# A layer norm feeding a 2-D Fourier filter and an MLP: features dealt to partitions, W1 on two queues, filter loads behind the normalized tiles

## The chip, the cores and the metric

The kernel runs on one core of a Trainium2 chip. The metric is the time of the program on the device in microseconds, the median of several runs. A profile of one execution gives a span (first to last instruction), which is a little shorter than the time.

## What is computed

Only A_x is used as input data (B_x is not read). With x of 2048 rows by 640:

```python
xn = _layernorm(x, axis=-1)                       # (x - mean) / sqrt(var + 1e-5), rows of 640
# A: spectral filter
X = jnp.fft.rfft2(xn.astype(jnp.float32), axes=(-2, -1)) * (w_r + 1j * w_i)     # 2048 x 321
yA = jnp.fft.irfft2(X, s=(2048, 640), axes=(-2, -1))
# B: MLP
h = _gelu(jnp.einsum("bsd,df->bsf", xn, w1) + b1)       # 640 -> 1536
yB = jnp.einsum("bsf,fd->bsd", h, w2) + b2              # 1536 -> 640
return x + yA + yB
```

All inputs and the output are bf16.

## The kernel before

**Tiles.** The 2048 rows are dealt to 16 tiles of 128: partition p holds rows 16p to 16p+15, tile c the c-th of each. X, the normalized and transposed xnT, W1, W2, the hidden gT, the filter Wf and the tables all stay in SBUF.

**Normalization, on VectorE, tile by tile.** Two statistics of 320 columns each (L483), an aggregate (L485), a small add (L492), the power -1/2 on POOL (L493), and the normalization itself (L511), which writes one of two pair buffers (`p_xn`, tiles 2k and 2k+1 share one). Tiles 0 to 5 are then transposed by TensorE (L527) and copied to xnT by VectorE or ScalarE; tiles 6 to 15 (`BYDMA`) by a transposing DMA on SyncE's queue (L518), which waits for the pair's normalizations. A pair buffer is free for the pair after next when its transposes have landed.

**Fourier part.** VectorE folds each pair with adds and subtractions (L539, L543); TensorE multiplies by gtab (the `aps` of a pair: ten matmuls, five a tile), and the result goes to XV. When all pairs are there, the forward transform along the width runs in six groups (etab; `bps`), then in four double pairs the small 32x32 matmuls with mtab (`cps`), the filter's products and sums on VectorE (L648, L652; they need the whole of Wf), the small matmuls with ntab (`dps`), and transposing DMAs (L673) back to XV. The inverse transform along the width (getab, `eps`) follows in six groups, VectorE unfolds (L704, L709), and one matmul with htab a tile adds the result to the tile's output.

**MLP.** The first layer runs in blocks of tiles, `BLOCKS`: tiles 0, 1, 2-3, 4-7, 8-11, 12-15. For each block and each of 12 chunks of 128 features, five matmuls accumulate in a PSUM bank, with the W1 columns as weights (the stationary operand) and xnT as the moving one, so 128, 256 or 512 columns wide; ScalarE applies Gelu with the bias column b1col (L581). The second layer (L732) takes gT as weights and W2 as the moving operand, 24 matmuls a tile (512 + 128 columns, 12 chunks). Eight tiles (`KEEP`) are summed early and parked in X or xnT (L741); for the others the htab matmul accumulates in the same bank. VectorE adds the rest (L750), and the outputs go out by an accumulating DMA on POOL (L757), over a copy of x that POOL has sent to the output ahead of them (issue at L376; it waits for the whole of Wf and for the last transposed tile), or for tiles 14 and 15 directly by SyncE (L754).

**Loads.** `load` (L375 to L380; all issues are shown at L376) puts every input on SyncE's queue: X tile 0, the first of W1's three parts (`W1P`: chunks 0-2, 3-6, 7-11), the identity, X tile 1, W1's second part, b1 (12 partitions of 128), X tiles 2-3, W1's third part, gtab, X tiles 4 to 15, W2 in four loads of three chunks, the tables etab, mtab, b2, ntab, getab, htab, and then the filter in 34 loads of 16 partitions with runs of 321 elements (`load_w`). b1 is turned into a column by a matmul with the identity (L469) and copied by ScalarE (L470).

**What sets the order.** Each engine's order is written out in `ORDER`, a text that a planner outside the kernel produced: operation number, engine letter, PSUM or buffer slots. `Sched.arrange` reads it, `Sched.sync` works out the semaphore waits from what each operation reads and writes (`deps`), and `Sched.emit` writes them. The arguments `prio`, `rate`, `issue`, `gate` and `hard` are for the planner: neither `sync` nor `emit` reads them.

Of the kernel before, what the change touches and what calls it, by code (L numbers as in the profile page):

```python
# [253 lines left out]
8s 2a 1d 3g 0d 4g 5g 6g 7p:0 9s 10s 11s 12s 13s 70d 14s 69d 15s 71d 16s 72a 17s 73a 74d 136d:0 18s 76d 137p:1 19s 139p:0 75d 140p:2 20s 141a 138d 77d 21s 257p:4 78d 258p 263p:5 79g  # L254
22s 264p 67p:6 269p:7 23s 68a 270p 81d 24s 266p:6 271a 83d 267p 259a 254p:7 25s 80d 268a 255p 260p:4 265a 261p 26s 142d 272p:6 256a 273p 82d 27s 262a 143p:5 145d:0 274a 28s 275p:4
146d 144a 276p 281p:7 84d 29s 284p:6 285p 277a 282p 147d:0 299p:5 30s 286a 300p 149d 293p:4 283a 294p 31s 311p:6 150d 301a 85d 312p 296p:7 148d 32s 295a 86d 297p 152p:0 87g 313a
89d 33s 317p:5 298a 318p 91d 151p 319a 305p:4 34s 154d:1 306p 153a 278p:6 100d 302p:7 155p:5 35s 99d 303p 279p 108d 304a 36s 280a 101d 156d 323p:7 307a 324p 37s 314p:6 157d 315p
325a 290p:5 291p 115d 316a 158p:4 38s 292a 124d 287p:7 288p 320p:6 39s 159d 321p 289a 308p:5 309p 322a 129d 338p:4 40s 310a 161d:0 356p:7 332p:6 96d 41s 357p 121d 341p:5 42s 358a
97d 342p 333p 160d 343a 359p:7 43s 98d 360p 334a 163d:1 102d 335p:5 165d 44s 103g 120d 361a 336p 350p:6 104d 337a 45s 351p 122d 184d:0 347p:7 352a 348p 128d 46s 326p:5 349a 164d
327p 185s 186d 353p:6 328a 354p 116d 344p:7 88d 355a 345p 339p 117d 47s 90d 346a 329p:5 92d 330p 340a 112d 187s 598p:6 331a 732d 613p:4 107d 48s 93d 109d 614p 94d 113d 95g 49s 123d  # L260
615p 114d 50s 172d:1 118d 169d 51s 119g 599p 125d 130d 126d 162d 52s 127g 170p:3 132d 166p:0 53s 175d:0 171a 167p 105d 600p 54s 168a 176d 106d 601p 55s 180d:0 110d 178d 111g 179d
# [529 lines left out]
```

## Time and profile before

| | |
|---|---|
| median of 3 runs | 160.04 us (159.53 to 160.74) |
| the profiled execution's time | 159.53 us |
| its span | 157.7 us |
| busy: TensorE (PE) | 146.2 us, 93% of the span |
| busy: VectorE (DVE) | 109.8 us, 70% |
| busy: ScalarE (ACT) | 77.5 us, 49% |
| busy: GpSimd (POOL) | 21.1 us, 13% |
| DMA | 20.71 MB, mean 131 GB/s |

Rows of the profile have the line of the kernel, the engine, the operation, output tile <- input tiles, the shape, and a count; a row of the order in time starts with start and duration in us and ends, in brackets, with the idle time just before it and what ended it. A row that merges several instructions has the time from the first's start to the last's end. PEld is TensorE's loading of weights, which overlaps its matmuls; SPq is SyncE's queue, whose rows are the issues of DMAs. The chain of waits follows the work that ended last back to the start.

### The profile page before, as it was taken

The numbers are of one execution on the slowest core, as the hardware profiler recorded it, in microseconds if no ns is written. First come the engines' busy times: TensorE is split into PE (matmuls) and PEld (weight loads), VectorE is DVE, ScalarE is ACT, GpSimd is POOL, SyncE is SP. The second block draws the span as 40 slices with busy tenths as digits, with TensorE's granted clock in tenths as the row PEclk, the third lists the DMA queues.
The fourth block names the chain that finished last, engine by engine and source line by source line (L and its number), as shares of the span: only waits on it lengthen the run. The fifth ranks groups of instructions, "written<-read, shape, count | busy, mean of one in ns | idle before, by whom it ended". The sixth has DMA issues, their size and how long they took to land.

```text
span 157.7 us, 4031 instructions
## 1 busy us (share of the span) xinstructions
PE 146.2 (93%) x1703; PEld 89.5 (57%) x1720; DVE 109.8 (70%) x234; ACT 77.5 (49%) x137; POOL 21.1 (13%) x34
## 2 busy tenths in 40 slices
PE   7879899967998799999999999999999999999993
PEld 7669887633454355544454554454456656665663
DVE  2549899998419544699866976961108997989552
ACT  3448976231487678696773553438663310220100
POOL 1001010522000004000000000000000247144520
PEclk9968999996999999999999999999999999999999
DMA  4999999998455537910062025044440079834953
GB/s 116 313 389 399 364 360 260 169 126 152 96 128 132 125 83 209 386 78 4 4 123 44 4 56 119 0 87 84 83 87 0 0 87 94 114 42 50 130 69 88
DMA packets 31337, 20.71 MB, mean 131 GB/s; under 512 B 19288, under 2 KB 29656, under 8 KB 31320
## 3 DMA queue, kind: packets, MB, share of 16 engines
q1 hardware_dynamic: 28728, 15.55, 40.5%
q0 software_dynamic: 2592, 4.92, 17.1%
q8 instruction: 13, 0.21, 0.6%
q14 instruction: 4, 0.03, 0.1%
HBM read 13.58 MB, written 5.24 MB: 119 GB/s over the span
## 4 chain that ended last, share of the span: by engine, by line
PE 69%; DVE 10%; SPq 9%; DMA 7%; issue 2%; ACT 1%
PE ps L385 69%; SPq L376 7%; DVE stats L483 4%; DMA W<-in_B_w_dram 4%; DMA xnT<-T 3%; SPq L518 2%; DVE T L539 1%; DVE T L543 1%; DVE T L511 1%; ACT XV L396 1%; DVE mv L485 1%; PE ps L527 1%; DVE xnT L719 1%; ACT gT L581 0%; DVE xnT L397 0%
## 5 line engine op out<-in xcount | busy, mean ns | idle before, releaser
L385 PE MATMUL ps<-xnT,W 128*128 128x512 bf16 (+2 forms) x360 | 60.0, 320 | 5.7 <-DMA xnT<-T 3.6
L385 PE MATMUL ps<-W,gT 128*128 128x128 bf16 (+3 forms) x382 | 54.8, 292 | 1.5 <-issue 1.1
L385 PEld LDWEIGHTS ps<-xnT,W 128*128 128x128 bf16 x360 | 30.4, 102 | 27.2 <-issue 5.8
L581 ACT ACTIVATE gT<-ps,b1col 128x512 bf16<-128x512 f32 (+2 forms) x72 | 36.3, 547 | 16.5 <-PE ps L385 15.5
L385 PEld LDWEIGHTS ps<-W,gT 128*128 128x128 bf16 x396 | 29.8, 98 | 22.6 <-issue 2.2
L757 POOL DMA_DIRECT2D out_dram<-W x14 | 12.2, 932 | 78.8 <-DVE W L750 78.8
L396 ACT ACTIVATE Wf<-ps 128x960 bf16<-128x960 f32 (+1 forms) x7 | 6.2, 893 | 24.3 <-PE ps L385 24.3
L483 DVE BATCH_NORM_STATS2 stats<-X 128x6 f32<-128x320 bf16 x32 | 14.2, 480 | 5.6 <-DMA X<-in_A_x_dram 5.6
L397 DVE CAST Wf<-ps 128x960 bf16<-128x960 f32 (+1 forms) x5 | 5.1, 1024 | 10.8 <-PE ps L385 10.8
L648 DVE TENSOR_TENSOR T<-Y,Wf 128x1288 bf16<-128x1288 bf16 x16 | 12.3, 822 | 0.0
L511 DVE TENSOR_SCALAR T<-X,mv,rstd 128x640 bf16<-128x640 bf16 x16 | 6.9, 435 | 5.6 <-DMA xnT<-T 5.6
L397 DVE CAST Xb<-ps 128x960 bf16<-128x960 f32 (+1 forms) x6 | 6.7, 1124 | 5.0 <-PE ps L385 5.0
L493 POOL TENSOR_TENSOR rstd<-ve,mhalf 128x2 f32<-128x2 f32 (+1 forms) x8 | 6.0, 750 | 31.1 <-DVE ve L492 31.1
L396 ACT ACTIVATE XV<-ps 128x1280 bf16<-128x1280 f32 (+1 forms) x8 | 9.3, 1156 | 1.5 <-PE ps L385 1.5
L543 DVE TENSOR_TENSOR T<-T 128x512 bf16<-128x512 bf16 (+1 forms) x32 | 8.7, 314 | 0.6 <-PE ps L385 0.6
L396 ACT ACTIVATE Y<-ps 128x644 bf16<-128x644 f32 x8 | 5.7, 708 | 6.9 <-PE ps L385 6.9
L397 DVE CAST Y<-ps 128x644 bf16<-128x644 f32 x8 | 6.6, 823 | 3.5 <-PE ps L385 3.4
L396 ACT ACTIVATE Xb<-ps 128x960 bf16<-128x960 f32 (+1 forms) x6 | 6.8, 1139 | 3.7 <-PE ps L385 3.7
L385 PE MATMUL ps<-getab,XV 32*128 32x160 bf16 (+1 forms) x128 | 7.6, 242 | 0.0
L741 DVE TENSOR_TENSOR X<-ps,b2bc 128x640 f32<-128x640 f32 x7 | 5.7, 821 | 2.4 <-PE ps L385 2.4
L539 DVE TENSOR_TENSOR T<-T 128x640 bf16<-128x640 bf16 x16 | 7.3, 482 | 0.1
L385 PEld LDWEIGHTS ps<-getab,XV 32*128 32x128 bf16 (+1 forms) x128 | 6.4, 147 | 1.6 <-DMA XV<-gtab 0.4
(49 smaller groups left out, 124.6 us busy)
## 6 DMA issues: line engine op xcount, KB each, us to landing
out_dram<-in_A_x_dram POOLq DMA_DIRECT2D x4, 640.0 KB, 7.1
W<-in_B_w_dram SPq DMA_DIRECT2D x5, 480.0 KB, 10.8
X<-in_A_x_dram SPq DMA_DIRECT2D x7, 320.0 KB, 9.2
out_dram<-W POOLq DMA_DIRECT2D x14, 160.0 KB, 3.7
Wf<-in_A_w_r_dram SPq DMA_DIRECT2D x15, 80.2 KB, 5.7
Wf<-in_A_w_i_dram SPq DMA_DIRECT2D x15, 80.2 KB, 2.7
W<-in_B_w_dram SPq DMA_DIRECT2D x1, 800.0 KB, 7.9
W<-in_B_w_dram SPq DMA_DIRECT2D x1, 640.0 KB, 6.3
```

The lines of the kernel that those rows point to most:

```text
L376: o = K.op([(q, 1.0 if q == "pool" else issue)], prio, lambda e, _: e.dma_start(dst, src), reads=reads, writes=[buf], after=after, dma=(nb ...
L385: ins = e.matmul(o_, lhsT=lw, rhs=rh, start=st, stop=sp_, skip_group_check=True)
L396: return e.activation(dst(), src(), ACT.Copy, scale=scale)
L397: return e.tensor_copy(dst(), src())
L483: st_ops.append(K.op([("dve", 0.393)], pr, lambda e, _, c=c, h=h: e.bn_stats(stats[:, c, 6 * h:6 * h + 6], view(X, c * D + H2 * h, [[1, H2 ...
L493: K.op([("pool", 0.65)], 400 + pr, lambda e, _, a=a, b=b: e.tensor_tensor(out=rstd[:, a:b], in0=ve[:, a:b], in1=mhalf[:, a:b], op=ALU.pow) ...
L511: o = K.op([("dve", 0.356)], pr, lambda e, _, c=c, n=n, xnv=xnv: e.tensor_scalar(out=xnv(n, 0, [[1, D]]), in0=view(X, c * D, [[1, D]]), sc ...
L539: K.op([("dve", 0.39)], pr, lambda e, _, k=k, op=op, xnv=xnv, x1v=x1v: e.tensor_tensor(out=x1v(H2 * k, [[D, 2], [1, H2]]), in0=xnv(0, 0, [ ...
L543: ring_ops.append(K.op([("dve", 0.333 if w == 128 else 0.136)], pr, lambda e, _, op=op, x1v=x1v, xfv=xfv, o_=o_, o0=o0, o1=o1, w=w: e.tens ...
L581: K.op([("act", act_us(128 * nt, 1) + 0.02)], pr + PRIO["gelu"], lambda e, _, c0=c0, nt=nt, fc=fc, hps=hps: e.activation(gT[:, fc, 128 * c ...
L648: filt_ops.append(K.op([("dve", 0.738)], pr, lambda e, _, k=k, Y=Y, TB=TB, pair=pair: e.tensor_tensor(out=view(TT, TB.slot * 8 * KP + k * ...
L757: last.append(K.op([("pool", 0.9)], 450, lambda e, _, c=c, os_=os_: e.dma_start(ov[:, c, :], view(W1, OST + os_.slot * D, [[1, D]]), accum ...
```

## The change

- Features are dealt to partitions differently: inside each of W1's three parts, which have 3, 4 and 5 chunks, chunk j of partition p is now feature 128a + p(b-a) + j, where a and b are the part's ends in chunks. W2 is loaded in three loads, in which a partition reads one run of 3, 4 or 5 rows of 640. b1 is loaded as a column, in three loads on POOL's queue, and widened to f32 by a copy on POOL. The matmul and the ScalarE copy for b1 are gone. The W1 columns that serve as weights of one matmul are now 3, 4 or 5 elements apart.
- W1's second and third parts are loaded by ScalarE's queue.
- On SyncE's queue the identity and X tile 1 come ahead of W1's first part; getab and htab come behind the filter loads.
- `FILTER` gives five filter loads (numbers 0, 8, 14, 20, 26) a gate on the normalization of tiles 7, 9, 11, 13 and 15.
- Some of the planner's rates differ, and `ORDER` is written anew for all engines.

The diff, with `ORDER` cut to its first lines:

```diff
 ORDER = """
-8s 2a 1d 3g 0d 4g 5g 6g 7p:0 9s 10s 11s 12s 13s 70d 14s 69d 15s 71d 16s 72a 17s 73a 74d 136d:0 18s 76d 137p:1 19s 139p:0 75d 140p:2 20s 141a 138d 77d 21s 257p:4 78d 258p 263p:5 79g
...
+8s 2a 1d 3g 0d 5g 4g 6g 7p:0 9s 22g 10s 20a 11s 24g 21a 12s 13s 69d 26g 14s 70d 15s 71d 76d 72a 16s 73a 74d 17s 136d:0 75d 18s 139p:1 140p:0 19s 77d 141a 78d 137p:2 23s 79g 138d
...
@@ -292,6 +292,7 @@
 CHAIN = "b0 b1 c00 c01 b2 c10 c11 d00 d01 b3 b4 c20 c21 d10 d11 b5 c30 c31 d20 d21 d30 d31".split()
 XASPLIT = [((0, 1, 2, 3, 4),)] * 7 + [((0, 1), (2, 3, 4))]
 WARM = (42, 10)
+FILTER = {7: 0, 9: 8, 11: 14, 13: 20, 15: 26}
 
 
 def bass_parallel_sum__spectral_gfnet__dense_activation_gelu__prompt_kernel(
@@ -311,8 +312,6 @@
     xv = A_x[0].rearrange("(p c) d -> p c d", c=16)
     ov = out[0].rearrange("(p c) d -> p c d", c=16)
     w1v = B_w1.rearrange("(c p) f -> p c f", p=128)
-    w2v = B_w2.rearrange("(c p) e -> p c e", p=128)
-    b1v = B_b1.rearrange("(c p) -> c p", p=128)
     b2v = B_b2.rearrange("(o e) -> o e", o=1)
 
     K = Sched(nc, ["sp", "pe", "act", "dve", "pool"])
@@ -336,7 +335,7 @@
         ntab = sb("ntab", [128, 2 * 3 * 32])
         getab = sb("getab", [128, 800])
         htab = sb("htab", [128, 16, 128])
-        b1t = sb("b1t", [NFC, 128])
+        b1t = sb("b1t", [128, NFC])
         b1col = sb("b1col", [128, NFC], F32)
         b2bc = sb("b2bc", [128, D])
         stats = sb("stats", [128, 16, 12], F32)
@@ -370,13 +369,12 @@
         p_xn, p_x1, p_xf, p_xb, p_y, p_t, p_z, p_u = Pool(2), Pool(1), Pool(2), Pool(2), Pool(2), Pool(2), Pool(2), Pool(3)
         p_yo, p_y2, p_yf, p_os = Pool(2), Pool(1), Pool(2), Pool(8)
 
-        queued = []
+        queued = {"sp": [], "act": [], "pool": []}
 
         def load(dst, src, buf, nbytes, after=(), reads=(), rate=400e3, q="sp", prio=400, issue=0.45, late=0.0, group=None):
             o = K.op([(q, 1.0 if q == "pool" else issue)], prio, lambda e, _: e.dma_start(dst, src), reads=reads, writes=[buf], after=after, dma=(nbytes, rate), late=late, group=group,
-                     hard=queued[-1:] if q == "sp" else [])
-            if q == "sp":
-                queued.append(o)
+                     hard=queued[q][-1:])
+            queued[q].append(o)
             return o
 
         def mms(lst):
...
+        w_ops = []
...
@@ -426,33 +425,32 @@
 
         def load_w1(j, prio, q="sp"):
             a, b = W1P[j]
-            load(view(W1, 128 * a, [[F, 5], [1, 128 * (b - a)]]), w1v[:, :, 128 * a:128 * b], B_w1s[j], 163840 * (b - a), q=q, prio=prio)
+            load(view(W1, 128 * a, [[F, 5], [1, 128 * (b - a)]]), w1v[:, :, 128 * a:128 * b], B_w1s[j], 163840 * (b - a), rate=330e3, q=q, prio=prio)
         pr = iter(range(999, 900, -1))
         load_x(0, 1, next(pr))
-        load_w1(0, next(pr))
         load(ident[:], const["I"], B_id, 32768, rate=200e3, prio=next(pr))
         load_x(1, 1, next(pr))
-        load_w1(1, next(pr))
-        load(b1t[:], b1v, B_b1, 3072, prio=next(pr))
+        load_w1(0, next(pr))
         load_x(2, 2, next(pr))
-        load_w1(2, next(pr))
         load(gtab[:], const["G"], B_g, 524288, prio=next(pr))
         for c in range(4, 16, 2):
             load_x(c, 2, next(pr))
-        for h in range(4):
-            load(W2[:, 3 * h:3 * h + 3, :], w2v[:, 3 * h:3 * h + 3, :], B_w2, F * D // 2, prio=next(pr), group="w2")
+        load_w1(1, 405, q="act")
+        load_w1(2, 404, q="act")
+        for a, b in W1P:
+            load(b1t[:, a:b], bass.AP(tensor=B_b1.tensor, offset=B_b1.offset + 128 * a, ap=[[b - a, 128], [1, b - a]]), B_b1t, 8192, q="pool", prio=460)
+            load(W2[:, a:b, :], bass.AP(tensor=B_w2.tensor, offset=B_w2.offset + 128 * a * D, ap=[[(b - a) * D, 128], [D, b - a], [1, D]]),
+                 B_w2b, (b - a) * D * 256, prio=next(pr), group="w2")
         load(etab[:], const["E"], B_e, 204800, prio=next(pr))
         load(mtab[:], const["M"], B_m, 65536, rate=200e3, prio=next(pr))
         load(b2bc[:], bass.AP(tensor=b2v.tensor, offset=b2v.offset, ap=[[0, 128], [1, D]]), B_b2b, 163840, prio=next(pr))
         load(ntab[:], const["N"], B_n, 49152, rate=200e3, prio=next(pr))
-        load(getab[:], const["GE"], B_ge, 204800, prio=next(pr))
-        load(htab[:].rearrange("p a b -> p (a b)"), const["H"], B_h, 524288, prio=next(pr))
         WP = 32 * KP
 
         def load_w(wsrc, p0, off, row, n, step):
-            load(bass.AP(tensor=Wf, offset=p0 * WP + off, ap=[[2 * WP, 16], [2 * KP, n], [1, 321]]),
+            w_ops.append(load(bass.AP(tensor=Wf, offset=p0 * WP + off, ap=[[2 * WP, 16], [2 * KP, n], [1, 321]]),
                  bass.AP(tensor=wsrc.tensor, offset=wsrc.offset + row * 321, ap=[[128 * 321, 16], [step * 321, n], [1, 321]]),
-                 B_w, 16 * 642 * n, after=[wpad], rate=250e3, issue=0.645, group="W", prio=next(pr))
+                 B_w, 16 * 642 * n, after=[wpad], rate=175e3, issue=0.645, group="W", prio=next(pr)))
         for ri, wsrc in enumerate((A_w_r, A_w_i)):
             for pp in range(2):
                 for qq in range(2):
@@ -465,9 +463,10 @@
                         else:
                             load_w(wsrc, p0 + 1, off, 64, 1, 1)
                             load_w(wsrc, p0 + 1, off + 2 * KP, 127, 7, -1)
-        B_b1ps, B_b1c = Buf("b1ps", psum), Buf("b1col")
-        pe([("32", 0.1)], 200, lambda: [(psb(B_b1ps.slot, [[1, NFC]]), b1t[:], ident[0:NFC, 0:NFC], True, True)], reads=[B_b1, B_id], writes=[B_b1ps])
-        K.op([("act", 0.2)], 200, lambda e, _: e.activation(b1col[:], psb(B_b1ps.slot, [[1, NFC]]), ACT.Copy), reads=[B_b1ps], writes=[B_b1c])
+        load(getab[:], const["GE"], B_ge, 204800, prio=next(pr))
+        load(htab[:].rearrange("p a b -> p (a b)"), const["H"], B_h, 524288, prio=next(pr))
+        B_b1c = Buf("b1col")
+        K.op([("pool", 0.2)], 455, lambda e, _: e.tensor_copy(b1col[:], b1t[:]), reads=[B_b1t], writes=[B_b1c])
 
         B_xnT = [Buf(f"xnT{c}") for c in range(16)]
         B_xa = [Buf(f"xa{c}") for c in range(8)]
@@ -513,8 +512,10 @@
                     reads=[B_x[c], B_rs[c]], writes=[xn, B_xn])
                 norm_ops.append(o)
                 if not c:
-                    st_ops[2].gate.append(o)
+                    st_ops[2].hard.append(o)
                 if c in BYDMA:
+                    if c in FILTER:
+                        w_ops[FILTER[c]].gate.append(norm_ops[-1])
                     ring_ops.append(K.op([("sp", 1.28)], 1500, lambda e, _, c=c, n=n, xnv=xnv: e.dma_start_transpose(xnT[:, c, :, :], xnv(n, 0, [[1, D]])),
                          reads=[B_xn, xn], writes=[B_xnT[c]], dma=(163840, 200e3)))
                     continue
@@ -573,8 +574,8 @@
                 w = [j for j, (a, b) in enumerate(W1P) if a <= fc < b][0]
                 part_ = []
                 for js in ((0, 1, 2), (3, 4)):
-                    part_ = [pe([("128", len(js) * mm_us(128 * nt))], pr + 0.01 * len(part_), lambda c0=c0, nt=nt, fc=fc, hps=hps, js=js: [
-                        (psb(hps.slot, [[1, 128 * nt]]), view(W1, F * j + 128 * fc, [[1, 128]]), xnT[:, c0:c0 + nt, j, :], j == 0, j == 4) for j in js],
+                    part_ = [pe([("128", len(js) * mm_us(128 * nt))], pr + 0.01 * len(part_), lambda c0=c0, nt=nt, fc=fc, hps=hps, js=js, w=w: [
+                        (psb(hps.slot, [[1, 128 * nt]]), view(W1, F * j + 128 * W1P[w][0] + fc - W1P[w][0], [[W1P[w][1] - W1P[w][0], 128]]), xnT[:, c0:c0 + nt, j, :], j == 0, j == 4) for j in js],
                         reads=[B_w1s[w]] + B_xnT[c0:c0 + nt], writes=[hps], hard=part_)]
                     l1_ops += part_
                     l1_of.setdefault(bi, []).extend(part_)
...
```

52 lines of the change are left out of this document (26 added, 26 removed).

## The prediction

> **What bounds the kernel now.** I read the chain of waits first, then the stretches, then each queue in order of time.
>
> ```profile
> PE 69%; DVE 10%; SPq 9%; DMA 7%; issue 2%; ACT 1%
> ```
>
> TensorE carries 69% of the chain, VectorE a tenth and SyncE's queue (SPq) 9%. Stretches (span; busy us and count of PE, PEld, DVE, ACT, POOL; granted clock; DMA share; GB/s):
>
> ```profile
> 9.00:12.50 3.50, 3.50 (x34) 3.19 (x35) 2.63 (x8) 2.09 (x8) 0.00 (x0) 0.56 1.05 391
> 33.90:36.50 2.60, 0.19 (x4) 0.01 (x1) 2.60 (x8) 0.00 (x0) 0.00 (x0) 1.00 1.16 196
> 36.50:40.50 4.00, 3.92 (x15) 1.84 (x16) 3.39 (x15) 1.72 (x2) 0.93 (x1) 0.57 0.51 93
> 57.16:117.40 60.24, 59.29 (x893) 29.48 (x899) 38.45 (x57) 37.37 (x67) 2.29 (x4) 1.00 0.36 91
> 117.40:155.40 38.00, 37.28 (x359) 24.44 (x365) 30.32 (x46) 6.84 (x8) 12.23 (x14) 1.00 0.53 66
> ```
>
> From 57.16 to 155.40 TensorE is full: 96.6 of 98.2 us. What an early change can win therefore lies before 57 us: a hole of 2.6 us at 33.9, then 4 us at a clock of 0.57 (4 x 0.43 = 1.7 us lost), and two waits that end at 48.81 and 52.72. TensorE in order of time (start, us; the wait ahead in brackets):
>
> ```profile
> 7.19 0.45 PE L385 MATMUL ps<-xnT,W 128*128 128x128 bf16 x5 [0.32 <-DVE xnT L397]
> 12.78 2.29 PE L385 MATMUL ps<-xnT,W 128*128 128x128 bf16 x35
> 18.62 7.55 PE L385 MATMUL ps<-xnT,W 128*128 128x128 bf16 x75
> 26.22 4.02 PE L385 MATMUL ps<-W,gT 128*128 128x128 bf16 x29
> 36.58 2.16 PE L385 MATMUL ps<-xnT,W 128*128 128x512 bf16 x5 [2.49 <-DMA xnT<-T]
> 45.78 0.72 PE L385 MATMUL ps<-gtab,T 128*128 128x128 bf16 x10
> 46.34 1.90 PE L385 MATMUL ps<-xnT,W 128*128 128x512 bf16 x8
> 48.81 0.72 PE L385 MATMUL ps<-gtab,T 128*128 128x128 bf16 x10 [0.57 <-DVE T L543]
> 52.72 1.89 PE L385 MATMUL ps<-xnT,W 128*128 128x512 bf16 x8 [1.11 <-DMA xnT<-T]
> 55.65 1.67 PE L385 MATMUL ps<-xnT,W 128*128 128x512 bf16 x7
> 57.16 0.97 PE L385 MATMUL ps<-etab,XV 128*128 128x160 bf16 x16
> 139.23 3.42 PE L385 MATMUL ps<-W,gT 128*128 128x512 bf16 x24
> 142.49 0.43 PE L385 MATMUL ps<-Wf,htab 128*128 128x512 bf16 x2
> ```
>
> The cause of the waits is SyncE's queue, where filter loads (L376, Wf) stand ahead of the transposing DMAs (L518):
>
> ```profile
> 19.48 9.99 SPq L376 DMA_DIRECT2D Wf<-in_A_w_r_dram  x14
> 31.50 1.28 SPq L518 DMA_TRANSPOSE xnT<-T  x1
> 34.10 8.12 SPq L376 DMA_DIRECT2D Wf<-in_A_w_i_dram  x11
> 55.42 1.24 SPq L376 DMA_DIRECT2D Wf<-in_A_w_i_dram  x2
> ```
>
> Tile 7 is sent at 31.50 and TensorE gets it at 36.58. Tiles 8 and 9 wait behind the eleven loads of 34.10, and VectorE, whose buffers they hold, stands for 5.59 us:
>
> ```profile
> 9.87 1.28 DVE L483 BATCH_NORM_STATS2 stats<-X 128x6 f32<-128x320 bf16 x3 [2.43 <-DMA X<-in_A_x_dram]
> 14.19 0.89 DVE L483 BATCH_NORM_STATS2 stats<-X 128x6 f32<-128x320 bf16 x2 [0.25 <-DMA X<-in_A_x_dram]
> 46.93 0.45 DVE L511 TENSOR_SCALAR T<-X,mv,rstd 128x640 bf16<-128x640 bf16 x1 [5.59 <-DMA xnT<-T]
> 65.68 2.30 DVE L648 TENSOR_TENSOR T<-Y,Wf 128x1288 bf16<-128x1288 bf16 x3
> ```
>
> **The change, part by part.** First, what it isn't: the hold of FILTER is a planner's gate, and gates make no semaphore. The built order has eight filter loads on SyncE right behind the tables, unheld, and the others between transposes, which hold them by place. The counts below are those of that order.
>
> *W1 and X.* The bytes ahead of tiles 4 and 5 are the same 3.5 MB, so I leave their landing at 14.19. Tile 1's normalization and pair 0's adds now come ahead of tile 2's statistics and fill the 2.43 us wait of 9.87. ScalarE's two DMA issues lie between its first table load and its wait for VectorE: no cost.
>
> *Tiles 6 and 7*, now normalized ahead of 4 and 5. Prices from the chain of waits (start, us):
>
> ```profile
> 23.36 0.40 DVE stats L483
> 23.76 0.32 DVE T L543
> 24.08 0.36 DVE T L511
> 31.27 0.39 DVE T L539
> 31.66 0.12 DVE mv L485
> 31.78 0.14 DVE T L543
> 44.24 2.66 DMA xnT<-T
> ```
>
> From tile 4's statistics (14.2): 17 statistics 6.8, five aggregates 0.6, one L539 0.4, three L543 0.6, two normalizations 0.7, a copy taken as one more 0.4, a small add 0.1: 9.6, so 23.8. SyncE's eight loads at 9.99/14 = 0.71 take 5.7; two tables fewer stand ahead of them than at 19.48, so they are out by 24. The transposes of 6 and 7 start at 24.2 and 25.5. Even with the 5 us that tile 7's took (31.50 to 36.58) both land by 30.5. Behind 23.8 VectorE has two statistics, four L539, five L543, two aggregates, two normalizations, and two wide additions estimated at 0.8 (twice a normalization), 6.2 us; then tiles 4 and 5, through TensorE and a copy ready near 32.5.
>
> *TensorE up to there.* First layer of tiles 0 to 3: 105 matmuls at 2.29/35 = 0.065, 6.8, and the 75 of 18.62, 7.55. Then 35 gtab and 25 transposing ones at (46.34-45.78)/10 = 0.056, 3.4, and two tiles of the second layer at 142.49-139.23 = 3.26, 6.5: 24.3 us. It starts near 7.4 (W1's first part now follows one more tile of X than at 7.19) and keeps the low clock of 9.0 to 12.5 (3.5 x 0.44 = 1.5): 33.2, later than 32.5, so no hole. Against 36.58 that is **3.4**; the low clock behind the hole goes, **1.7**; ten more gtab matmuls are done by then, **0.6**.
>
> *The later transposes.* Tile 8 goes out at 27.7, 9 at 30.4, 10 (behind eight loads) at 37.3, 11 at 39.3, which lands 2.66 later at 42.0. TensorE wants it after 39 wide matmuls at (57.16-55.65)/7 = 0.216 and 30 gtab ones, at 43.3; VectorE reaches its wait for it at 42.5. So the waits of 48.81 and 52.72 go, **1.7**. Together 7.4. The stage of 57.16 then starts near 49.5.
>
> *The filter's end.* Transposes of 14, 15, 12, 13 and two loads bring SyncE to 47.2, twelve loads to 55.7. In the old kernel the last issue ended at 56.66, and the copies that wait for every filter began 2.1 later:
>
> ```profile
> 58.80 2.29 POOL L376 DMA_DIRECT2D out_dram<-in_A_x_dram  x4 [20.60 <-DMA Wf<-in_A_w_i_dram]
> out_dram<-in_A_x_dram POOLq DMA_DIRECT2D x4, 640.0 KB, 7.1
> ```
>
> So now 57.8. The first product came 8.5 behind the stage of 57.16 (65.68), so it is wanted at 58.0. The cover is thin; I charge **0.6**.
>
> *b1* drops a matmul and a ScalarE copy, and adds on POOL three loads in runs of 6 to 10 bytes and a copy, ahead of the powers for tiles 2 and up. No such load is in the trace. From below nothing; from above three issues at 2.29/4 and the landing of a large POOL copy, 7.1: the first Gelu near 10, and TensorE up to 2 us late. I take 0, since the loads are small.
>
> *W2 in long runs* gives TensorE nothing: it reached W2 at 26.22 without a wait, and gets there near 24.5 behind two tables' fewer bytes.
>
> *W1 read at steps of 3 to 5 as weights.* The nearest rows are the two transforms, one with packed weights (etab), one at step 16 (getab):
>
> ```profile
> L385 PEld LDWEIGHTS ps<-getab,XV 128*128 128x128 bf16 x64 | 4.8, 145 | 1.1 <-DMA XV<-gtab 0.4 <-DVE W L750 0.2
> L385 PEld LDWEIGHTS ps<-etab,XV 128*128 128x128 bf16 x64 | 4.5, 98 | 1.6 <-DVE Xb L397 0.7 <-DVE Y L397 0.3 <-ACT T L396 0.2
> 59.21 1.31 PE L385 MATMUL ps<-etab,XV 128*128 128x160 bf16 x24
> 120.07 1.37 PE L385 MATMUL ps<-getab,XV 128*128 128x160 bf16 x24
> ```
>
> A load takes 47 ns more, 24 matmuls only 0.06 us more. The wide matmul's 0.216 hides it; the 180 narrow ones pay between 0 and 47 ns. I take 4, the group's 0.06 over its 12 full-height matmuls less a little: **0.7**. On this the Trainium skill, page "TensorE: Matmul & The Clock Gate", has two rules: "LDWEIGHTS (loading the stationary operand)" gives 128 columns 107 ns, and "Weight-path perf modes" lets the fast load run for strided columns too. An estimate from that page by the first: 120 narrow matmuls at 107 in place of 56 cost 6 us, the time is about 160; by the second nothing, 153.7. The rows at step 16 bear out the second.
>
> **Sum.** 7.4, less 0.6, 0.7, and 0.5 for the wait ahead of the last transform (its last four transposing DMAs take 4 x 1.28 + 2.66 = 7.8, and nine quarter tiles at 0.82, 7.3, stand there to cover them): 5.6. The profiled execution took 159.53 (span 157.7), the lowest of three; from the median, 160.04, I forecast **154.4**.
>
> **Rivals.** (1) Slower: the strided load sets the pace of the 180 narrow matmuls between 7 and 25 us. At 145 ns each they take 26.1 in place of 14.4; less 6.3, 165.4. It decides from 6300/180 = 35 ns a load on. For it: the record of 145; against it: the 0.06. (2) The filter comes last: the last loads land 6 us behind their issue in place of 2.1, products start at 61.7, and 3.7 are given back: 158.1. For it: a cover of 0.2; against it: TensorE has first-layer work to do meanwhile. (3) The win is spent again: the rest of the order is re-dealt too, and the 98 us that now hold 1.6 of waits hold 7: 160. For it: VectorE is at 30.3 of the last 38.0, so a worse order there shows at once; against it: the same operations in much the same turn.
>
> **Chances.** Forecast 0.62, with a range of its own from 152 (no thin cover, cheap weights, W1 sooner) to 157 (b1's 2 us); (2) 0.13; (3) 0.11; (1), with any other loss, 0.14. About 1% is what a measurement of this kernel tells from no change, so 158.4 and 161.6 divide the cases: faster 0.75, same 0.11, slower 0.14. The range, 151 to 160, leaves (1) out.
>
> **What would show it.** TensorE's order of time: wide first-layer matmuls from about 33, no low clock near 37, the etab stage from about 49.5. SyncE's: a transpose near 24. VectorE: no 5 us wait on xnT. If narrow matmuls take over 0.075 each, the weights' price is wrong; if the first product comes later than 59, the filter's; if all that holds and the end does not move, it is (3).

## The result, and the profile after

The changed kernel takes **155.76 us** (median of 4 runs, 155.53 to 156.15) against 159.99 (4 runs of before beside it, 159.53 to 160.74): ratio 0.973, 95% interval 0.969 to 0.978. The profiled executions have spans of 153.7 and 157.7 us. So 4.2 us are gone, where 5.6 had been forecast. A run more than 1.5% above the fastest of its kernel counts as slow and is left out of the ratios, though not of the medians; the traces shown of transposes_ahead, before_both and w1_act_late are of slow runs.

The stretches of the changed kernel, with the columns as shown of before:

```profile
9.00:12.50 3.50, 2.91 (x29) 2.65 (x30) 2.60 (x9) 0.75 (x2) 0.72 (x2) 0.57 1.04 392
33.90:36.50 2.60, 2.60 (x29) 1.86 (x28) 2.32 (x8) 1.07 (x2) 0.00 (x0) 1.00 0.61 127
36.50:40.50 4.00, 4.00 (x24) 2.22 (x23) 4.00 (x15) 1.82 (x3) 0.69 (x1) 1.00 0.46 111
52.43:117.40 64.97, 64.72 (x954) 33.79 (x954) 43.98 (x69) 37.85 (x64) 2.14 (x4) 1.00 0.47 107
```

The hole of 33.9 is full (2.60 of 2.60), and behind it the clock is 1.00 where it was 0.57. The low clock of 9.0 to 12.5 has stayed. TensorE in order of time:

```profile
9.14 0.28 PE L528 MATMUL ps<-ident,T 128*128 128x128 bf16 x2 [3.45 <-DVE T L510]
11.09 1.03 PE L383 MATMUL ps<-xnT,W 128*128 128x128 bf16 x8 [0.45 <-DVE xnT L395]
12.46 4.10 PE L383 MATMUL ps<-xnT,W 128*128 128x128 bf16 x62
19.12 8.46 PE L383 MATMUL ps<-xnT,W 128*128 128x256 bf16 x93 [0.62 <-ACT xnT L394]
36.11 2.97 PE L383 MATMUL ps<-xnT,W 128*128 128x512 bf16 x13
52.43 0.97 PE L383 MATMUL ps<-etab,XV 128*128 128x160 bf16 x16
111.62 1.07 PE L383 MATMUL ps<-getab,XV 128*128 128x160 bf16 x16 [0.25 <-DMA XV<-T]
```

The two waits that ended at 48.81 and 52.72 have no counterpart. The stage with etab starts at 52.43 (57.16 before), 4.73 us sooner, with as many wide matmuls of the first layer (64) done by then as in before. Behind it both kernels are nearly full: the changed one takes 101.3 us from there to its end and before 100.5, so most of what is won at the stage is kept, and the span falls by 4.0. From the first wide matmul to that stage the change takes 16.32 us (36.11 to 52.43) and before 20.58 (36.58 to 57.16): 4.26 are won there, and only 0.47 ahead of it. But the start is late: nothing for 3.45 us until 9.14, and the first layer begins at 11.09, where 7.4 had been forecast and before had 7.19. SyncE's queue:

```profile
12.88 8.38 SPq L375 DMA_DIRECT2D Wf<-in_A_w_r_dram  x8
26.73 2.62 SPq L519 DMA_TRANSPOSE xnT<-T  x2
49.82 8.53 SPq L375 DMA_DIRECT2D Wf<-in_A_w_i_dram  x12
```

The filter loads start 6.6 us sooner than at 19.48, end at 21.26, and the queue then stands until the transposes of tiles 6 and 7 go out at 26.73 (29.51 and 31.50 before; 24.2 and 25.5 forecast): now VectorE is late, not the queue.

Why the start is late is seen in the issues of the first two microseconds, with the size and the time from issue to landing; first of the changed kernel:

```profile
0.77 1.03 ACTq L375 DMA_DIRECT2D W<-in_B_w_dram  x2
1.66 0.43 SPq L375 DMA_DIRECT2D X<-in_A_x_dram  x1
W<-in_B_w_dram ACTq DMA_DIRECT2D x1, 640.0 KB, 4.7
W<-in_B_w_dram ACTq DMA_DIRECT2D x1, 800.0 KB, 8.1
X<-in_A_x_dram SPq DMA_DIRECT2D x1, 160.0 KB, 6.4
W<-in_B_w_dram SPq DMA_DIRECT2D x1, 480.0 KB, 8.1
```

and the same two SyncE loads (tile 1 of X, W1's first part) in the kernel before:

```profile
X<-in_A_x_dram SPq DMA_DIRECT2D x1, 160.0 KB, 3.7
W<-in_B_w_dram SPq DMA_DIRECT2D x1, 480.0 KB, 4.2
```

ScalarE sends 1.44 MB at 0.77, while its first table load (0.73 to 2.01) runs. Tile 1 of X, issued at 1.66, lands at 8.0, and W1's first part at 10.2 (issued near 2.1). VectorE has tile 1's first statistics ahead of tile 0's normalization, so it waits:

```profile
8.04 0.49 DVE L482 BATCH_NORM_STATS2 stats<-X 128x6 f32<-128x320 bf16 x1 [3.38 <-DMA X<-in_A_x_dram]
8.63 0.45 DVE L510 TENSOR_SCALAR T<-X,mv,rstd 128x640 bf16<-128x640 bf16 x1
61.00 2.31 DVE L649 TENSOR_TENSOR T<-Y,Wf 128x1288 bf16<-128x1288 bf16 x3
```

Tile 0 is normalized at 8.63; in before that was

```profile
4.83 0.45 DVE L511 TENSOR_SCALAR T<-X,mv,rstd 128x640 bf16<-128x640 bf16 x1
```

### The profile page after: what moved, and what is told of

It reads as the page before. It is cut to its first block, busy times and chain, and to the rows that moved or that the text cites. A ratio compares the mean times of both kernels' runs of the same rounds, so it can differ in the third digit from the quotient of the medians.

```text
span 153.7 us, 4048 instructions
## 1 busy us (share of the span) xinstructions
PE 145.3 (95%) x1719; PEld 91.5 (60%) x1719; DVE 111.0 (72%) x240; ACT 74.9 (49%) x130; POOL 23.0 (15%) x38
## 4 chain that ended last, share of the span: by engine, by line
PE 79%; DMA 6%; SPq 5%; DVE 5%; ACT 2%; issue 1%
PE ps L383 78%; SPq L674 5%; DMA X<-in_A_x_dram 4%; DMA XV<-T 2%; DVE T L649 2%; PE ps L528 1%; DVE Z L653 1%; ACT XV L394 1%; SPq L375 1%; DVE gtab L395 1%; DVE U L395 1%; DVE X L742 0%; ACT Y L394 0%; ACT xnT L394 0%; DVE stats L482 0%
## 5 line engine op out<-in xcount | busy, mean ns | idle before, releaser
L383 PE MATMUL ps<-xnT,W 128*128 128x512 bf16 (+2 forms) x360 | 58.8, 312 | 1.1 <-ACT xnT L394 0.6
L383 PE MATMUL ps<-W,gT 128*128 128x512 bf16 (+3 forms) x396 | 57.2, 295 | 0.0
L582 ACT ACTIVATE gT<-ps,b1col 128x512 bf16<-128x512 f32 (+2 forms) x72 | 35.7, 550 | 16.0 <-PE ps L383 15.5
L383 PEld LDWEIGHTS ps<-xnT,W 128*128 128x128 bf16 x360 | 31.8, 115 | 18.8 <-issue 3.4
L649 DVE TENSOR_TENSOR T<-Y,Wf 128x1288 bf16<-128x1288 bf16 x16 | 12.5, 823 | 0.0
L395 DVE CAST Xb<-ps 128x960 bf16<-128x960 f32 (+1 forms) x5 | 5.9, 1179 | 9.0 <-PE ps L383 9.0
L394 ACT ACTIVATE Xb<-ps 128x960 bf16<-128x960 f32 (+1 forms) x7 | 7.7, 1116 | 4.0 <-PE ps L383 4.0
L395 DVE CAST Y<-ps 128x644 bf16<-128x644 f32 x7 | 5.8, 828 | 4.0 <-PE ps L383 4.0
L394 ACT ACTIVATE Y<-ps 128x644 bf16<-128x644 f32 x9 | 6.3, 708 | 3.5 <-PE ps L383 3.5
L710 DVE TENSOR_TENSOR Wf<-Wf 128x960 bf16<-128x960 bf16 (+1 forms) x12 | 6.9, 596 | 0.8 <-PE ps L383 0.7
L705 DVE TENSOR_TENSOR Wf<-Wf 128x960 bf16<-128x960 bf16 (+1 forms) x12 | 6.8, 597 | 0.9 <-ACT Wf L394 0.7
L653 DVE TENSOR_TENSOR Z<-T 128x644 bf16<-128x644 bf16 x16 | 6.9, 485 | 0.4 <-PE ps L383 0.4
```

Source lines behind the costliest of these rows:

```text
L383: ins = e.matmul(o_, lhsT=lw, rhs=rh, start=st, stop=sp_, skip_group_check=True)
L394: return e.activation(dst(), src(), ACT.Copy, scale=scale)
L395: return e.tensor_copy(dst(), src())
L582: K.op([("act", act_us(128 * nt, 1) + 0.02)], pr + PRIO["gelu"], lambda e, _, c0=c0, nt=nt, fc=fc, hps=hps: e.activation(gT[:, fc, 128 * c ...
L649: filt_ops.append(K.op([("dve", 0.738)], pr, lambda e, _, k=k, Y=Y, TB=TB, pair=pair: e.tensor_tensor(out=view(TT, TB.slot * 8 * KP + k * ...
L653: K.op([("dve", 0.402)], pr, lambda e, _, TB=TB, Z=Z, r=r, op=op: e.tensor_tensor(out=view(Zb, Z.slot * 4 * KP + r * KP, [[2 * KP, 2], [1, ...
```

## The experiments

The kernels ran in three groups, each beside its own runs of before (medians 160.42, 160.33 and 159.43; the changed kernel ran in none of them, its ratio is that of the result): w1_on_sync, norm0_first, weights_packed and transposes_ahead in the first; before_hold, before_both, w1_act_late and old_sync_order in the second; the other four in the third. Each ratio is to the runs of its own group. Two of the texts on record give a run as "152.7 us": that is the first experiment. In `ORDER`, words 185 and 187 are the transposes of tiles 6 and 7, 198 and 200 those of 8 and 9, 211 and 213 of 10 and 11, 224 and 226 of 12 and 13, 237 and 239 of 14 and 15; 20 and 21 are W1's second and third part, and 32 (before: 33) and up the filter loads. Of a changed turn on SyncE only SyncE's words are shown, and of the other edits to `ORDER` only the words around them; "33s to 46s" stands for the words between.

### All of W1 on SyncE (w1_on_sync)

```diff
-8s 2a 1d 3g 0d 5g 4g 6g 7p:0 9s 22g 10s 20a 11s 24g 21a 12s 13s 69d
+8s 2a 1d 3g 0d 5g 4g 6g 7p:0 9s 22g 10s 11s 20s 24g 12s 21s 13s 69d
```

> The changed kernel, but W1's second and third parts back on SyncE's queue (the second behind the first part, the third behind X tiles 2-3). Theory A (late start): in the changed kernel X tile 1 lands only at 8.0 us because ScalarE's two W1 loads, out at 0.77, take the DMA engines first; tile 0's normalization stands behind tile 1's statistics, and the first layer starts at 11.1. TensorE is full from 19 us on, so a sooner start moves the end. Then X tile 1 lands near 4.3, the first layer starts near 7.3, and the time is about 152.7 (3 us under 155.8). Theory B (something else sets the pace: VectorE's chain to 49.5 us or the filter loads that land at 61): the start moves but the time falls by less than 1 us, 155 to 155.8.

**152.70 us** (152.45 to 152.86), ratio 0.950 (0.944 to 0.955): 3 us faster than the changed kernel, and the lowest median of all that ran. The two SyncE loads, and TensorE, of this run:

```profile
X<-in_A_x_dram SPq DMA_DIRECT2D x1, 160.0 KB, 2.9
W<-in_B_w_dram SPq DMA_DIRECT2D x1, 480.0 KB, 4.1
7.09 0.63 PE L384 MATMUL ps<-xnT,W 128*128 128x128 bf16 x8 [0.45 <-DVE xnT L396]
9.42 3.61 PE L384 MATMUL ps<-xnT,W 128*128 128x128 bf16 x57 [1.09 <-DMA W<-in_B_w_dram]
33.52 2.97 PE L384 MATMUL ps<-xnT,W 128*128 128x512 bf16 x13
49.85 0.97 PE L384 MATMUL ps<-etab,XV 128*128 128x160 bf16 x16
PEclk9999999999999999999999999999999999999999
```

Tile 1 lands in 2.9 us and W1's first part in 4.1 where the change had 6.4 and 8.1, and the first layer starts at 7.09. The wait for W1's second part, which the issue by ScalarE would have spared, is 1.09 us: less than the 4 us that it cost. No slice has a low clock, not even near 9 us, where before and the change have one. And this kernel comes near the times of the forecast: wide matmuls at 33.52 (33.2), the etab stage at 49.85 (49.5). That is in part luck: the forecast has 1.5 us for a low clock near 9 us, which this run doesn't have, and no waits, where this run waits 1.09 us for W1's second part and 0.78 for gtab (at 13.81).

### Tile 0's normalization ahead of tile 1's statistics (norm0_first)

On VectorE, word 76 (statistics of tile 1) is put behind 136 (normalization of tile 0):

```diff
-70d 15s 71d 76d 72a 16s 73a 74d 17s 136d:0 75d
+70d 15s 71d 72a 16s 73a 74d 17s 136d:0 76d 75d
```

> The changed kernel, but on VectorE tile 0's reciprocal and normalization stand ahead of tile 1's first statistics. Theory A: tile 0 is normalized near 5.4 in place of 9.1 and its transposes follow, but W1's first part lands only at 10.2 behind ScalarE's loads, so the first layer starts at 10.2 in place of 11.1 and the time falls by at most 0.9: 155 to 155.8. If the order on VectorE alone made the late start, it would start near 7.3 and the time be 152.7. Theory B: 155.8.

156.0 us (155.13 to 156.29), ratio 0.969 (0.963 to 0.976), no gain on the change. Tile 0 is normalized at 5.21, but TensorE then waits 3.29 us for W1's first part and starts the first layer at 10.10. That is 1 us sooner than in the change, yet the row of 93 first-layer matmuls shown above at 19.12 begins at 19.60 here: in this trace the clock is 0.50 from 9 to 14 us and 0.74 from 14 to 17, where the change has 0.62, 0.50 and 0.87 up to 14 and then 1.00. The order on VectorE that made it wait for tile 1 is only the first of two things that the late landing reaches.

### One part of W1 on ScalarE (one_w1_act)

```diff
-9s 22g 10s 20a 11s 24g 21a 12s 13s
+9s 22g 10s 20a 11s 24g 12s 21s 13s
```

> The changed kernel with W1's second part (640 KB) still on ScalarE's queue at 0.77 and its third part (800 KB) on SyncE. Theory A, what is lost is in proportion to the bytes ahead: tile 1 of X lands at 5.5 to 6.5 us (4.5 without, 8.02 with both), the first layer starts at 8 to 9, about 154 us. Theory C, any load on the second queue costs the whole: tile 1 near 8, 155.5 us. Theory D, one part ahead is hidden because it is wanted early anyway: 152.4 to 153 us.

153.56 us (152.25 to 153.84), ratio 0.962 (0.957 to 0.968). Its loads, and where TensorE starts:

```profile
X<-in_A_x_dram SPq DMA_DIRECT2D x1, 160.0 KB, 4.4
W<-in_B_w_dram SPq DMA_DIRECT2D x1, 480.0 KB, 6.3
9.35 1.03 PE L384 MATMUL ps<-xnT,W 128*128 128x128 bf16 x8 [0.45 <-DVE xnT L396]
```

With none, 640 KB and 1,440 KB ahead, tile 1 takes 2.9, 4.4 and 6.4 us, W1's first part 4.1, 6.3 and 8.1, and the first layer starts at 7.09, 9.35 and 11.09. All three grow with the bytes ahead, as theory A has it. The time follows (spans 150.9, 151.6 and 153.7 us; ratios 0.950, 0.962 and 0.973), though not in proportion. By the spans W1's second part on ScalarE costs 0.7 us (2.0 by the ratios of the two groups) though the start is 2.3 late: the waits of 1.09 and 0.78 are spared.

### W1 on ScalarE, but late (w1_act_late)

```diff
-9s 22g 10s 20a 11s 24g 21a 12s 13s 69d 26g 14s 70d 15s 71d 76d 72a 16s
+9s 22g 10s 11s 24g 12s 13s 69d 26g 14s 70d 15s 71d 76d 72a 20a 21a 16s
```

> The changed kernel with ScalarE's two loads of W1 issued behind its first activation (it waits for tile 0's statistics, near 4.3 us) and not at 0.77. Theory A, the 1.44 MB that went out ahead held back tile 1 of X and W1's first part: tile 1 lands near 4.6 us, tile 0 is normalized near 5.1 and the first layer starts near 7.1; W1's second part comes near 10.5, about 1 us later than from SyncE: 152.7 to 154.2 us. Theory C, a second hardware queue costs by itself, however late: tile 1's landing or W1's first part is late again and the time stays near 155.8 us.

163.24 us (161.86 to 165.02), ratio 1.020 (1.010 to 1.030): slower than before by 1 to 3%, and by neither theory's number.

```profile
7.42 0.63 PE L384 MATMUL ps<-xnT,W 128*128 128x128 bf16 x8 [0.45 <-DVE xnT L396]
15.73 5.30 PE L384 MATMUL ps<-xnT,W 128*128 128x128 bf16 x57 [7.12 <-DMA W<-in_B_w_dram]
26.27 10.94 PE L384 MATMUL ps<-xnT,W 128*128 128x128 bf16 x108 [4.12 <-DMA W<-in_B_w_dram]
```

The start is early, as theory A has it. But the two parts, issued at 4.3 behind gtab and tiles of X that SyncE has sent already and beside those that it goes on sending, take 11.3 and 21.4 us (6.7 and 8.6 from SyncE in the run of 152.7), and TensorE waits for them 7.12 and 4.12 us. So by these times to landing it works both ways: what goes out first on either queue delays the other's loads. I had put their landing near 10.5 from the size alone.

### The identity on ScalarE's queue (ident_on_act)

```diff
-8s 2a 1d 3g 0d 5g 4g 6g 7p:0 9s 22g 10s 11s 20s 24g 12s 21s 13s
+8s 2a 9a 1d 3g 0d 5g 4g 6g 7p:0 22g 10s 11s 20s 24g 12s 21s 13s
```

> The run of 152.7 us (all of W1 on SyncE) with the 32 KB of the identity on ScalarE's queue, so that everything behind it on SyncE goes out 0.46 us sooner. W1's second part was waited for 1.09 us at 9.42 and gtab 0.78 us at 13.81, so both waits shrink by 0.46: 152.0 to 152.3 us. Rival, tile 0's chain sets the start and the waits follow bytes, not issues: 152.7 us.

153.03 us (152.32 to 154.35), ratio 0.961 (0.953 to 0.968): no gain. The waits near 9 and 13 us did shrink (0.71 for a Gelu, which had itself waited 2.03 us for b1's column, and 0.42 for gtab stand there), but W2 is now waited for:

```profile
25.66 1.79 PE L384 MATMUL ps<-W,gT 128*128 128x512 bf16 x12 [1.49 <-DMA W<-in_B_w_dram]
```

The third of W2's loads takes 16.5 us to land, 13.9 in the run of 152.7. The DMA engines are full in both (a share of 1.02 to 1.08 from 7 to 17 us), and I take that as the reason why issues 0.46 us sooner win nothing; the rival's number was nearer.

### Packed weights (weights_packed)

The first layer reads W1's columns side by side, so that its features no longer match b1 and W2, whose order stays: the output is another function, the work the same.

```diff
-view(W1, F * j + 128 * W1P[w][0] + fc - W1P[w][0], [[W1P[w][1] - W1P[w][0], 128]])
+view(W1, F * j + 128 * fc, [[1, 128]])
```

> The changed kernel, but the first layer reads W1's columns as weights side by side, in the order of the memory, while b1 and W2 keep the dealt order: the same work, with features that do not belong together. If weights at a step of 3 to 5 elements cost nothing, 155.8 within 0.4, and the narrow first-layer matmuls keep 0.056 to 0.063 us. By the prediction's term (4 ns on 180 narrow ones) 155.1. If each narrow matmul were paced by a slow load, several us less, 150 or so.

155.72 us (155.30 to 155.91), ratio 0.968 (0.961 to 0.975), as the change. The weight loads of the changed kernel and of this one (busy us, mean ns):

```profile
L383 PEld LDWEIGHTS ps<-xnT,W 128*128 128x128 bf16 x360 | 31.8, 115 | 18.8 <-issue 3.4 <-ACT gT L582 0.9 <-DVE xnT L395 0.7
```

```profile
L383 PEld LDWEIGHTS ps<-xnT,W 128*128 128x128 bf16 x360 | 29.4, 101 | 21.0 <-issue 3.4 <-ACT gT L582 1.0 <-DVE xnT L395 0.7
```

The record of a load is 14 ns longer at steps of 3 to 5, but the matmuls keep their pace. With the weights side by side:

```profile
19.54 8.45 PE L383 MATMUL ps<-xnT,W 128*128 128x256 bf16 x93 [0.62 <-ACT xnT L394]
36.51 2.97 PE L383 MATMUL ps<-xnT,W 128*128 128x512 bf16 x13
```

At the steps the same rows take 8.46 and 2.97 us (the row of 93 merges narrow matmuls and those of 256 columns), and the 15 narrow matmuls just ahead of the 93 take 1.00 us in both. (The 62 narrow ones before those ran in part at a low clock in both kernels, so they can't be compared.) By the Trainium skill ("TensorE: Matmul & The Clock Gate", "Weight-path perf modes") the fast load runs for strided columns too; the runs agree in that the steps cost no time, 155.76 with them and 155.72 without.

### W2 in rows again (w2_rows)

On top of the run of 152.7, W2 is loaded in rows of 640 for each feature, so that the second layer pairs features that do not belong together and only the time counts:

```diff
-ap=[[(b - a) * D, 128], [D, b - a], [1, D]]
+ap=[[D, 128], [128 * D, b - a], [1, D]]
```

> The changed kernel with all of W1 on SyncE (152.7 us), W2 loaded in rows of 1,280 bytes for each feature again, while W1 and b1 keep the dealt order, so the second layer pairs features wrongly and only the time counts. Theory A, the long runs win SyncE's issue time alone (6.67 us for four loads before, 1.45 for three after): the filter loads end near 26.5 and not 22.0, tile 6 goes out near 26.5 and lands in time for 33.5, so the time stays within 0.5 us, 152.5 to 153.2. Theory B, the turn on SyncE is tight and every transpose behind comes 2.4 us later: a new wait, 154 to 155.5 us.

153.59 us (153.08 to 154.20), ratio 0.964 (0.959 to 0.969); span 151.3 against 150.9. SyncE's queue:

```profile
8.55 2.65 SPq L376 DMA_DIRECT2D W<-in_B_w_dram  x3
11.24 5.81 SPq L376 DMA_DIRECT2D etab<-c_E  x1
18.71 6.05 SPq L376 DMA_DIRECT2D Wf<-in_A_w_r_dram  x8
24.81 3.03 SPq L520 DMA_TRANSPOSE xnT<-T  x2
```

The issue behind W2's three takes 5.81 us (1.64 in the run of 152.7), and the filter loads start at 18.71, not at 14.69. Tile 6's transpose goes out at 24.81 instead of 24.12, TensorE has one new wait of 0.52 us at 32.16, and the median stands between the two theories' numbers. The long runs free 4 us of SyncE's queue, and the turn has slack for most of that.

### The turn on SyncE alone

**Later transposes first (transposes_ahead).** In the kernel before, the turn from 185s on:

```diff
-185s 47s 187s 48s to 60s 224s 61s 226s 62s 198s 200s 211s 213s 63s 64s 239s 237s 65s 66s
+185s 47s 187s 48s 49s 224s 226s 50s 198s 200s 51s to 56s 211s 213s 57s 58s 239s 237s 59s to 66s
```

> The kernel before, with one edit: on SyncE's queue the transposing DMAs of tiles 8 to 15 stand ahead of most filter loads (two loads after tile 7's come those of 12 and 13, one load later 8 and 9, six loads later 10 and 11, two later 14 and 15, the rest behind). By the prediction's terms the hole of 33.9 to 36.6 and the low clock behind it stay, VectorE's 5.6 us wait and TensorE's waits of 0.57 and 1.11 go: about 158.3. Rival: SyncE's order alone makes the whole gain: 155.8. A second rival: VectorE's wait cost nothing, since TensorE has first-layer work to do: 160.

158.82 us (156.51 to 161.35), ratio 0.980 (0.967 to 0.993). The interval holds the expectation (158.3 is 0.987 of this group's before) and the first rival (155.8 is 0.971) alike, so the time sizes nothing. The trace shows what the edit does: the hole stays (3.01 us ahead of 36.44), VectorE no longer stands 5.59 us on xnT, and the waits of 0.57 and 1.11 on TensorE are gone.

**Only tiles 6 and 7 sooner (before_hold).**

```diff
-33s to 46s 185s 47s 187s 48s
+33s to 40s 185s 187s 41s to 48s
```

> The kernel before, with one thing changed: on SyncE the transposes of tiles 6 and 7 stand behind eight filter loads and not behind 14 and 15. Their tiles are normalized by 23.4 and 24.4 in the trace of before, so they go out at 25.2 and 26.5 and land by 31.5. Theory A, the terms of the forecast add up: the hole at 33.9 (2.5 us) and the low clock behind it (1.7 us) go, about 155.8 us. Theory B, the later transposes (tiles 8 to 13) keep their places behind the next thirteen loads, so TensorE only meets its waits at 48.81 and 52.72 earlier and waits longer there: about 159.5 to 160 us, with the etab stage still near 57.

163.21 us (162.75 to 163.67), ratio 1.023 (1.017 to 1.029): slower, by 1.7 to 2.9%: theory B and more. TensorE and VectorE:

```profile
50.70 1.23 PE L385 MATMUL ps<-gtab,T 128*128 128x128 bf16 x10 [6.29 <-DVE T L543]
48.81 0.45 DVE L511 TENSOR_SCALAR T<-X,mv,rstd 128x640 bf16<-128x640 bf16 x1 [7.33 <-DMA xnT<-T]
```

The hole of 33.9 is gone and comes back ten microseconds later, larger: VectorE waits 7.33 us for tiles 12 and 13's transposes to free its buffers, TensorE 6.29 us for VectorE, and the clock is at 0.50 behind it, from 50.7 to 56. The etab stage starts at 60.5.

**Both (before_both).**

```diff
-33s to 46s 185s 47s 187s 48s to 60s 224s 61s 226s 62s 198s 200s 211s 213s 63s 64s 239s 237s 65s 66s
+33s to 40s 185s 187s 41s to 49s 224s 226s 50s 198s 200s 51s to 56s 211s 213s 57s 58s 239s 237s 59s to 66s
```

> The kernel before with SyncE's order alone changed: tiles 6 and 7's transposes behind eight filter loads, and those of 12, 13, 8, 9, 10, 11, 15, 14 ahead of most of the others. By both theories no hole, no low clock and no long VectorE wait: 4.2 and 1.7 less, about 154.1 us, etab stage near 51.5; what is over that is the filter's later end or a new wait on VectorE.

159.61 us (median of 10 runs, 156.82 to 161.55), ratio 0.991 (0.984 to 0.997). In the trace the first hole is gone, but TensorE waits for tiles 10 and 11, which stand behind the six loads 51 to 56 (out at 47.28 and after):

```profile
51.15 3.57 PE L385 MATMUL ps<-xnT,W 128*128 128x512 bf16 x8 [4.55 <-DMA xnT<-T]
```

**Each transpose where its tile is ready (before_resort).**

```diff
-33s to 46s 185s 47s 187s 48s to 60s 224s 61s 226s 62s 198s 200s 211s 213s 63s 64s 239s 237s 65s 66s
+33s to 40s 185s 187s 41s 224s 226s 42s 43s 198s 200s 44s to 47s 211s 213s 48s to 58s 239s 237s 59s to 66s
```

> The kernel before with SyncE's turn alone changed, this time each transpose right where its tile is normalized: eight filter loads, tiles 6 and 7, a load, 12 and 13, two loads, 8 and 9, four loads, 10 and 11, eleven loads, 15 and 14, eight loads. The run with six loads ahead of 10 and 11 met a 4.55 us wait of TensorE for a transposed tile. Theory A, SyncE's turn alone holds the gain: no wait of TensorE over 1 us on xnT or VectorE, etab stage near 52, about 154 to 156 us. Theory B, VectorE's order has to change with it (tiles 12 and 13 stand ahead of 8 and 9, which are normalized only near 34 us): a wait of 2 us or more stays, 157 to 159 us.

161.39 us (160.81 to 163.78), ratio 1.012 (1.007 to 1.017). SyncE's last filter loads, VectorE and TensorE:

```profile
57.06 5.09 SPq L376 DMA_DIRECT2D Wf<-in_A_w_i_dram  x8
64.96 2.31 DVE L648 TENSOR_TENSOR T<-Y,Wf 128x1288 bf16<-128x1288 bf16 x3 [4.05 <-DMA Wf<-in_A_w_i_dram]
68.46 0.77 PE L385 MATMUL ps<-Xb,mtab 32*32 32x322 bf16 x32 [3.68 <-DVE Xb L397]
```

The etab stage starts at 52.3, almost as early as in the changed kernel, with waits of 0.41 and 1.64 us ahead of it. But SyncE stood from 30.8 to 34.7 for tiles 12 and 13, the last filter load goes out 5.5 us later than in before (62.15 against 56.66), VectorE waits 4.05 us for the filter, TensorE 3.68, the clock drops again, and all is given back. This is rival (2) of the prediction, in another kernel. Neither theory named it. The changed kernel's turn could not be tried as it is with the old order on VectorE: that writes tiles 10 and 11 into the buffers of 12 and 13, whose transposes would then stand behind theirs.

**The old turn in the new kernel (old_sync_order).** On top of the run of 152.7, with the old counts of filter loads ahead of each transpose; the transposes keep the new order of tiles:

```diff
-32s to 39s 185s 187s 40s 198s 41s 42s 200s 43s to 50s 211s 51s 213s 239s 237s 52s 226s 53s 224s 54s to 65s
+32s to 45s 185s 46s 187s 47s to 59s 198s 60s 200s 61s 211s 213s 239s 237s 62s 63s 226s 224s 64s 65s
```

> The changed kernel with all of W1 on SyncE (the run of 152.7 us), and on SyncE the old turn of filter loads and transposes: 14 loads, tile 6, one load, tile 7, thirteen loads, then the rest. Theory A, the hold is what took the hole away: hole and low clock return, 4 us or more, 156.9 us or above. Theory B, W2's four loads of 6.67 us of issue became three of 1.45 us, so the filter loads start near 14.7 and not 19.5, and tile 6 goes out near 26.3 even behind 14 of them, in time for 33.5: no hole, only the later waits (1.7) come back, about 154.4 us.

162.46 us (161.68 to 164.41), ratio 1.017 (1.008 to 1.025): all of the gain and more is lost. Its queue and TensorE:

```profile
13.41 13.55 SPq L375 DMA_DIRECT2D Wf<-in_A_w_r_dram  x14
33.14 0.81 PE L528 MATMUL ps<-ident,T 128*128 128x128 bf16 x10 [1.76 <-DVE T L510]
46.25 0.71 PE L383 MATMUL ps<-gtab,T 128*128 128x128 bf16 x5 [5.75 <-DVE T L544]
```

The number is on theory A's side, the reason only half: tile 6 went out at 27.01, near the 26.3 of theory B, and at 33 only 1.76 us were lost. The large wait is that for tiles 8 and 9 behind thirteen loads, by way of VectorE's buffers.

## Why the forecast came close, and where it was wrong

- **The side and the mechanism held.** The hole (TensorE idle for 2.5 us), the low clock behind it and the two later waits are gone; the 0.57 and 1.11 us that ended at 48.81 and 52.72 have nothing in their place. The terms for what follows the hole, 1.7, 0.6 and 1.7, measured 4.26 together. The win needs the new turn of SyncE's queue: with the old one the new kernel is slower than before (old_sync_order). The turn alone does not give it: three turns with the transposes of tiles 6 and 7 sooner, on the old kernel, left 0.991 to 1.023 of the time.
- **The step that failed is "ScalarE's two DMA issues lie between its first table load and its wait for VectorE: no cost", and with it "it starts near 7.4".** I counted the issue on ScalarE and not the bytes on the DMA engines. They went out 0.9 us ahead of tile 1 of X, which then took 6.4 us to land and not 2.9, and W1's first part 8.1 and not 4.1 (against w1_on_sync, where only these two loads are moved). The wide matmuls started at 36.11, not at 33.2: of the 3.4 us forecast for the hole 0.47 were won. Undone alone, 152.70 us, with stage times near the forecast's (33.52, 49.85). By the Trainium skill ("DMA: Bandwidth & Descriptors", "Issuing engines are not separate DMA queues") DMAs of all issuing engines run on the same 16 engines and interleave; the runs with none, one and two parts agree, at 2.9, 4.4 and 6.4 us for tile 1.
- **The charges of 1.8 were too high.** Strided weights, 0.7 charged: nothing (weights_packed). The last transform's wait, 0.5: 0.25, at 111.62. The filter's cover, 0.6: nothing, since the stage came later. It was as thin as said: the last filter issue ended at 58.35, the copies that wait for all of it began at 61.19, the first product at 61.00 without a wait; with all of W1 on SyncE the product came at 58.62, and a kernel whose last filter issue ended 0.8 us later (w2_rows) waited 0.19 for them. Behind the etab stage the change takes 0.7 us more than before, where 1.8 were charged. So the stage, 4.7 us sooner and not 7.4, was 2.7 too rosy and the rest 1.1 too dark: a part cancels, by luck, and 1.6 are left (4.0 us by the spans, where 5.6 were forecast; by the medians 155.8 against 154.4).
- **Two sums were off.** 57.16 less 7.4 is 49.8, not 49.5, and rival (2) adds its 3.7 to a forecast that already holds 0.6 for the same wait: 157.5, not 158.1.
- **"W2 in long runs gives TensorE nothing"** missed SyncE: four loads took 6.67 us of its queue, three now 1.84 (1.45 in w1_on_sync), so the filter loads start at 12.88 and not at 19.48, and I had counted only two tables less. That this room is what lets transposes go sooner without making the filter late is not shown: in the old kernel, without it, other turns gained 2% at most, or lost, but there VectorE's order is the old one too. Taken alone in the new turn (w2_rows) W2's part of the room, 4 us, is worth 0.4 us by the spans, and up to 2.3 by the ratios of the two groups (0.964 less 0.950, of 160).
- **Which tiles are ready.** "Tiles 6 and 7, now normalized ahead of 4 and 5" is no change: the trace of before has both done by 24.4, with the queue late. The transposes that I took for tiles 8 and 9 at 42.27 and 44.24 are those of 12 and 13; 8 to 11 follow at 46.20. The wait on buffers that I built on it is right (before_hold made it 7.33 us).
- **b1 as a column** cost nothing in the changed kernel: its loads took 5.7 to 6.2 us to land, and the first Gelu, at 11.84, waited for TensorE. That is only because the start was late. In w1_on_sync the first Gelu waits 1.88 us for b1's column, until 8.21; TensorE waits for W1's second part until 9.42 anyway, but in ident_on_act and old_sync_order 0.71 us for a Gelu is left.
- **The rivals.** (1) did not occur, (2) did not occur here but does in before_resort, and of (3) little is seen: behind the etab stage the changed kernel takes 0.7 us more than before, where (3) has 5.4.

What stays open: why W2's third load lands later in ident_on_act than in the run of 152.7, what the 0.7 us behind the etab stage are beyond the wait of 0.25, and how much of the win the new order on VectorE holds, since the new turn can't be had without it.

## What to carry to other kernels

A second engine's queue was no second set of DMA engines here: a big load issued early there delayed the small ones that the first matmul needs (2.9 us to 6.4 for tile 1 of X), so order the first megabytes by when they are wanted, whoever issues them. A queue that carries loads and transposes is one resource with several deadlines: moving one sooner moves others later, and the first wait that is taken away (before_hold) may come back larger behind it, so cost every later item of the queue, and the issue time of each, before counting a hole as won. Write down the time at which each stage should begin: here a part of two errors cancelled in the total, and only the stage times showed them.

## What the runs showed of the hardware that was not expected

- A load's time to landing can grow two and a half times by what shares the DMA engines: W1's third part took 8.6 us from SyncE in its turn, 8.1 from ScalarE at 0.77, and 21.4 from ScalarE at 4.3.
- The clock can drop behind a short gap of TensorE, and the length of the last gap doesn't say when. It fell behind 2.49 us (36.58 before, granted 0.57 for 4 us), 3.45 (9.14 after) and 2.30 (7.19 in one_w1_act), but also behind two of 1.07 and 1.05 in a row (7.43 and 8.93 in before_hold: 0.50 from 9 to 11), and not behind 2.28 (9.57 in before_both: 1.00 up to 19). What it cost where it fell, estimated from its length: 1.5 to 1.7 us in before, about 2.7 in before_hold (0.50 from 50.7 to 56).
- It doesn't drop in every execution of a kernel. Of the 27 executions of before in the three groups, 8 have a mean granted clock of 1.00 (158.5 to 160.9 us) and 9 one of 0.98, as the profiled one has (159.7 to 162.0). So the forecast's 1.7 us for the low clock behind the hole is what the profiled execution lost; by these times the median loses less.
- ScalarE's DMA issues at 0.77 ran beside its table load of 0.73 to 2.01.
